# Splitting the P·V matmuls of a decode attention kernel into four column groups, with a new input load, an earlier w2 load and filler matmuls

## The chip, the cores and the metric

The kernel runs on one core of a Trainium2 chip. The metric is the device time of one execution in microseconds (us). A run gives several executions of the changed kernel and of the kernel before it on the same chip. "Span" is the time from the first to the last instruction in a profile; in the two profiled executions it is about 1.8 us shorter than the device time.

The engines are PE (TensorE, matmuls), PEld (its weight loads), DVE (VectorE), ACT (ScalarE), POOL (GpSimd) and SP (SyncE, which here issues the transfers).

## The reference

One decode step mixes attention over a cached K and V with a small MLP, through a gate. B = 2 batches, H = 32 heads, 4096 cached positions, head size 128, model size 512, all in bf16.

```
g = sigmoid((x * gate_w).sum(-1))                 # x: 2 x 1 x 512
q = x @ wq                                        # 32 heads of 128
p = softmax(q . k_cache * 128**-0.5)              # k_cache: 2 x 32 x 4096 x 128
a = (p . v_cache) @ wo                            # v_cache the same size as k_cache
b = relu(x @ w1) @ w2                             # w1: 512 x 1376, w2: 1376 x 512
out = g * a + (1 - g) * b                         # 2 x 1 x 512
```

K and V are 134 of the 145 MB that must be read, and each element is used once.

## The kernel before

The 64 (batch, head) problems run as 32 pairs. A pair's two heads lie on the two halves of the 128 partitions. For each pair, DVE multiplies the K tile by q, and PE sums the products over the head size: 16 matmuls against the identity accumulate 128 columns into 8, and DVE sums those. ACT takes the exponential and writes it to PT_sb. Then comes P·V.

```python
def mult(s):                                    # DVE, 4.4 us
    prod = prodpool.tile([P, NC, Dh], bf16, name="prod")
    nc.vector.tensor_tensor(out=prod, in0=k_t.pop(s), in1=q, op=ALU.mult)

def red(s):                                     # PE, 16 matmuls of 512 columns
    for j in range(Dh // RW):
        nc.tensor.matmul(ps, lhsT=ident, rhs=prod[:, :, j * RW : (j + 1) * RW], ...)

def pv(s):                                      # PE, 16 matmuls of 512 columns
    o_ps = opool.tile([M, JB * Dh], fp32, name="o_ps")          # M = 8 rows
    for q in range(NQ):                                          # NQ = 16
        nc.tensor.matmul(
            o_ps,
            lhsT=PT_sb[:, s % PT_SLOTS, q * JB : (q + 1) * JB, :].rearrange("p j t -> p (j t)"),
            rhs=vt[:, q * JB : (q + 1) * JB, :],
            start=(q == 0), stop=(q == NQ - 1),
        )
# evac(s): ACT scales o_ps by gate / softmax sum into osb (fp32)
# comb(s): PE adds the rows of osb with a 0/1 matrix, 4 fp32 matmuls
```

The stationary operand of a P·V matmul has only 8 columns (4 chunks of keys, two heads), so one PE pass over 512 columns of V uses 8 of 128 columns of the array.

The order of issue matters at the end of the run, since the work of an engine is queued in this order:

```python
for s in range(NP + 3):                         # NP = 32
    if s < NP: mult(s)
    if 3 <= s < NP + 2: sums(s - 2)
    if s >= 3: evac(s - 3); comb(s - 3); unpack(s - 3)
    if s < NP: red(s)
    if 1 <= s <= NP: scores(s - 1)
    ...
    if 2 <= s < NP + 2: pv(s - 2)
    if s >= 3: wo_mm(s - 3)
    ...
    load_k(s + 3); load_v(s + 1)
    if s + 1 == NP - 1: load_wo(NG - 1); load_w2()
mlp_o()                                         # 11 matmuls with w2
# then two casts (DVE, ACT) and the output DMA
```

So when the last product (pair 31) is ready, PE still has to do reduction 31, P·V of pairs 29, 30 and 31 with an evacuation and a combination after each, 8 matmuls with wo and 11 with w2.

The softmax here doesn't subtract the row's maximum and nothing guards it: scores larger than these inputs give would overflow.

Of the kernel before, what the change touches and what calls it, by code (L numbers as in the profile page):

```python
# [9 lines left out]
ACT = mybir.ActivationFunctionType  # L10
ALU = mybir.AluOpType
# [6 lines left out]
JB = 4  # L18
PT_SLOTS = 4
# [3 lines left out]
def kernel(  # L23
# [13 lines left out]
    nc = tc.nc  # L37
    bf16 = mybir.dt.bfloat16
# [11 lines left out]
    DC = D // P  # L50
    NC = Sk // HP
    NQ = NC // JB
    M = 2 * JB
    NP = B * H // 2
    NG = H // GH
    GP = GH // 2
# [62 lines left out]
    def load_v(s):  # L119
# [7 lines left out]
        v_t[s] = t  # L127

    load_k(0)
    xT = consts.tile([P, B, DC], bf16, name="xT")  # L130
    nc.sync.dma_start(out=xT, in_=A_x[:, 0, :].rearrange("b (p c) -> p b c", c=DC))
    gwT = consts.tile([P, DC], bf16, name="gwT")
    nc.sync.dma_start(out=gwT, in_=gate_w.rearrange("(p c) -> p c", c=DC))  # L133
    load_wq(0)
    load_k(1)
    load_k(2)
# [1 line left out]

    ident = consts.tile([P, P], bf16, name="ident")
    make_identity(nc, ident[:])  # L140
    sel = consts.tile([M, JB, 32], fp32, name="sel")
    nc.gpsimd.memset(sel, 0.0)
    nc.gpsimd.affine_select(
        out=sel,
        in_=sel,
        compare_op=ALU.not_equal,
        fill=1.0,
        base=0,
        pattern=[[-2, JB], [-1, 2], [0, DA]],
        channel_multiplier=1,  # L150
    )
    half = consts.tile([P, M], fp32, name="half")
    nc.vector.memset(half, 0.0)
    nc.vector.memset(half[:HP, 0::2], 1.0)
    nc.vector.memset(half[HP:, 1::2], 1.0)
    PT_sb = consts.tile([P, PT_SLOTS, NC, 2], bf16, name="PT_sb")
    nc.vector.memset(PT_sb, 0.0)
    umask = consts.tile([P, DA], fp32, name="umask")
    nc.vector.reduce_sum(
# [3 lines left out]
    OT_sb = consts.tile([P, NG, DR, B], bf16, name="OT_sb")  # L163
    w1_sb = consts.tile([P, DC, Dff], bf16, name="w1_sb")
    w2_sb = consts.tile([P, FC, D], bf16, name="w2_sb")
    xb = consts.tile([P, B, DC, HP], bf16, name="xb")
    for b in range(B):
        nc.vector.tensor_copy(  # L168
            out=xb[:, b], in_=xT[:, b, :].unsqueeze(2).to_broadcast([P, DC, HP])
        )  # L170
    gwb = consts.tile([P, DC, P], bf16, name="gwb")
    nc.vector.tensor_copy(out=gwb, in_=gwT.unsqueeze(2).to_broadcast([P, DC, P]))
    a_ps = apool.tile([B, D], fp32, name="a_ps")
    g_sb = consts.tile([P, B], fp32, name="g_sb")
    omg = consts.tile([P, B], fp32, name="omg")
# [1 line left out]
    def make_qb(g):  # L177
        wq = wq_t[g // WQG].rearrange("p c (i t d) -> p c t i d", t=2, d=Dh)
        i0 = (g % WQG) * GP
        qb = qbpool.tile([P, B, GP, Dh], bf16, name="qb")  # L180
        for b in range(B):
            ps = mmp.tile([P, GP * Dh], fp32, name="mm")
            for t in range(2):
                for c in range(DC):
                    nc.tensor.matmul(  # L185
                        ps[t * HP : (t + 1) * HP, :],
                        lhsT=xb[:, b, c, :],
                        rhs=wq[:, c, t, i0 : i0 + GP, :],
                        start=(c == 0),
                        stop=(c == DC - 1),  # L190
                    )
            nc.scalar.copy(out=qb[:, b], in_=ps.rearrange("p (i d) -> p i d", d=Dh))  # L192
        qb_t[g] = qb
# [23 lines left out]
    def scores(s):  # L217
        sc = smalls.tile([P, NC], fp32, name="sc")
        nc.vector.reduce_sum(out=sc, in_=red_t.pop(s), axis=AX.X)  # L219
        for t in range(2):  # L220
            r = slice(t * HP, (t + 1) * HP)
            nc.scalar.activation(  # L222
                out=PT_sb[r, s % PT_SLOTS, :, t],
                in_=sc[r],
                func=ACT.Exp,
                scale=inv_sqrt_dh,
                accum_out=partials[r, s : s + 1],
            )

    def sums(s):  # L230
        gs = gsp.tile([M, 1], fp32, name="gs")
        nc.tensor.matmul(gs, lhsT=half, rhs=partials[:, s : s + 1], start=True, stop=True)  # L232
        rsg = smalls.tile([M, 1], fp32, name="rsg")
        nc.vector.reciprocal(out=rsg, in_=gs)  # L234
        b = pair(s)[1]
        nc.vector.tensor_tensor(out=rsg, in0=rsg, in1=g_sb[:M, b : b + 1], op=ALU.mult)  # L236
        rsg_t[s] = rsg

    def pv(s):
        vt = v_t.pop(s)  # L240
        o_ps = opool.tile([M, JB * Dh], fp32, name="o_ps")
        for q in range(NQ):
            nc.tensor.matmul(  # L243
                o_ps,
                lhsT=PT_sb[:, s % PT_SLOTS, q * JB : (q + 1) * JB, :].rearrange(
                    "p j t -> p (j t)"
                ),
                rhs=vt[:, q * JB : (q + 1) * JB, :],
                start=(q == 0),
                stop=(q == NQ - 1),  # L250
            )
        o_t[s] = o_ps

    def evac(s):
        osb = smalls.tile([M, JB, Dh], fp32, name="osb")
        nc.scalar.activation(  # L256
            out=osb,
            in_=o_t.pop(s).rearrange("m (j d) -> m j d", d=Dh),
            func=ACT.Copy,
            scale=rsg_t.pop(s),  # L260
        )
        osb_t[s] = osb
# [42 lines left out]
    def gate():  # L305
        ps = mmp.tile([P, GP * Dh], fp32, name="mm")
        z = ps[:, :B]
        for c in range(DC):
            nc.tensor.matmul(
                z, lhsT=gwb[:, c, :], rhs=xT[:, :, c], start=(c == 0), stop=(c == DC - 1)  # L310
            )
        ge = consts.tile([P, B], fp32, name="ge")
        nc.scalar.activation(out=ge, in_=z, func=ACT.Exp, scale=-1.0)
        nc.vector.tensor_scalar_add(ge, ge, 1.0)
        nc.vector.reciprocal(out=g_sb, in_=ge)
        nc.vector.tensor_scalar(omg, g_sb, -1.0, 1.0, op0=ALU.mult, op1=ALU.add)
# [3 lines left out]
    def mlp_h():  # L320
        ps = mmp.tile([P, GP * Dh], fp32, name="mm")
        h_ps = ps[:, : FC * B].rearrange("p (f b) -> p f b", b=B)
        w1m = w1_sb[:, :, : FF * P].rearrange("p c (q f) -> p c f q", f=FF)
        for fc in range(FC):
            fs = P if fc < FF else FREM
            for c in range(DC):
                nc.tensor.matmul(  # L327
                    h_ps[:fs, fc, :],
                    lhsT=w1m[:, c, fc, :] if fc < FF else w1_sb[:, c, FF * P :],
                    rhs=xT[:, :, c],  # L330
                    start=(c == 0),
                    stop=(c == DC - 1),
                )
        for b in range(B):
            nc.scalar.activation(
                out=hT[:, b, :FF], in_=h_ps[:, :FF, b], func=ACT.Relu, scale=omg[:, b : b + 1]
            )
            if FREM:
                nc.scalar.activation(
                    out=hT[:FREM, b, FF:],  # L340
                    in_=h_ps[:FREM, FF:, b],
                    func=ACT.Relu,
                    scale=omg[:FREM, b : b + 1],
                )

    W2_CUTS = [0, 4, 8, FF]

    def load_w2():
        if FREM:
            nc.sync.dma_start(out=w2_sb[:FREM, FF, :], in_=B_w2[FF * P :, :])  # L350
        view = B_w2[: FF * P].rearrange("(p f) j -> p f j", f=FF)
        for f0, f1 in zip(W2_CUTS, W2_CUTS[1:]):
            nc.sync.dma_start(out=w2_sb[:, f0:f1, :], in_=view[:, f0:f1, :])

    def mlp_o():
        order = ([FF] if FREM else []) + list(range(FF))
        for f in order:
            fs = P if f < FF else FREM
            nc.tensor.matmul(  # L359
                a_ps,  # L360
                lhsT=hT[:fs, :, f],
                rhs=w2_sb[:fs, f, :],
                start=False,
                stop=(f == order[-1]),
            )

    make_qb(0)
    for s in range(NP + 3):
        if s < NP:
            mult(s)  # L370
        if 3 <= s < NP + 2:
            sums(s - 2)
        if s >= 3:
            evac(s - 3)
            comb(s - 3)
            unpack(s - 3)
        if s < NP:
            red(s)
        if 1 <= s <= NP:
            scores(s - 1)  # L380
        if s == 1:
            gate()
        if s == 2:
            sums(0)
        if 2 <= s < NP + 2:
            pv(s - 2)
        if s >= 3:
            wo_mm(s - 3)
        if s == 14:
            mlp_h()  # L390
        if s % PPG == PPG - 2 and (s + 2) // PPG < NG:
            make_qb((s + 2) // PPG)
        if s == 9:
            load_wq(1)
        if s % PPG == 3 and s < NP - PPG:
            load_wo(s // PPG)
        if s == 5:
            nc.sync.dma_start(out=w1_sb, in_=B_w1.rearrange("(p c) f -> p c f", c=DC))
        load_k(s + 3)
        load_v(s + 1)  # L400
        if s + 1 == NP - 1:
            load_wo(NG - 1)
            load_w2()
    mlp_o()

    res = consts.tile([B, D], bf16, name="res")
    nc.vector.tensor_copy(out=res[:, : D // 2], in_=a_ps[:, : D // 2])
# [32 lines left out]
```

## Time and profile before

| | before |
|---|---|
| median time (16 executions) | 362.88 us (361.46 to 364.41) |
| profiled execution | 362.03 us, span 360.2 us |
| mean granted PE clock | 0.948 |
| last K tile in use by DVE | from 326.1 us |
| last w2 piece landed (issue 331.6 plus 15.7 to landing) | about 347.3 us |

The page of the profile, the busy table and the table of 40 slices of the span (9.0 us each; a digit is the busy share in tenths, PEclk the granted clock in tenths):

```profile
PE 299.3 (83%) x1499; PEld 134.4 (37%) x1499; DVE 175.5 (49%) x156; ACT 50.8 (14%) x175; POOL 1.2 (0%) x8
...
PE   0364999998998966979799999999799999999976
...
PEclk9989899998999995998679999999999999999998
DMA  7999999999999999999999999999999999999930
GB/s 283 440 422 428 435 426 419 431 418 435 427 428 424 412 435 428 428 428 428 424 431 428 427 426 428 426 426 428 429 426 426 431 429 422 428 431 423 396 119 0
```

PE is the busiest engine by its share, but the DMA row is full from the second slice to the 38th, at about 427 GB/s. The Trainium skill, "DMA: Bandwidth & Descriptors" (Specifications), gives 435 GB/s as the fabric ceiling; the slices from the second to the 37th read 412 to 440 GB/s, so the trace agrees to about one per cent. Only the last two slices, 18 us, have little or no DMA.

Groups of instructions, same page (line, engine, operation, shapes, count, busy us and mean ns of one, idle time before and what ended it):

```profile
L201 DVE TENSOR_TENSOR prod<-kt,qb 128x8192 bf16<-128x8192 bf16 x32 | 141.3, 4419 | 75.4 <-DMA kt<-in_A_k_cache_dram 68.4
L208 PE MATMUL red<-prod,ident 128*128 128x512 bf16 x512 | 127.7, 408 | 15.4 <-DVE prod L201 15.4
L243 PE MATMUL o_ps<-vt,PT_sb 128*8 128x512 bf16 x512 | 115.7, 379 | 0.0
```

P·V keeps PE as busy as the reduction does. DVE waits 68 us for K tiles, which says again that the transfers set the pace.

The chain of waits in the last 35 us (start, length, what; read downward in time):

```profile
330.73 3.56 PE red L208 x16
334.29 3.55 PE o_ps L243 x16
...
338.67 1.06 PE comb L271 x8
339.72 3.55 PE o_ps L243 x16
...
344.10 1.06 PE comb L271 x8
345.15 3.56 PE o_ps L243 x16
...
348.79 0.69 ACT osb L256
...
349.52 1.07 PE comb L271 x8
...
351.28 3.00 PE a_ps L297 x8
354.28 2.96 PE a_ps L359 x11
```

No DMA stands in it. Three P·V groups (o_ps) of 3.55 us each, one after the other, and then the matmuls with wo and w2 (a_ps), end ten microseconds after the last byte of input has landed. One window of this tail (columns: window, length, busy us and count for PE, PEld, DVE, ACT, POOL, then the granted clock, DMA share and GB/s) shows the wo matmuls at half clock:

```profile
352.00:353.00 1.00, 1.00 (x4) 0.33 (x3) 0.00 (x0) 0.00 (x0) 0.00 (x0) 0.50 0.00 0
```

### The profile page before, as it was taken

The numbers are of one execution on the slowest core, as the hardware profiler recorded it, in microseconds if no ns is written. First come the engines' busy times: TensorE is split into PE (matmuls) and PEld (weight loads), VectorE is DVE, ScalarE is ACT, GpSimd is POOL, SyncE is SP. The second block draws the span as 40 slices with busy tenths as digits, with TensorE's granted clock in tenths as the row PEclk, the third lists the DMA queues.
The fourth block names the chain that finished last, engine by engine and source line by source line (L and its number), as shares of the span: only waits on it lengthen the run. The fifth ranks groups of instructions, "written<-read, shape, count | busy, mean of one in ns | idle before, by whom it ended". The sixth has DMA issues, their size and how long they took to land.

```text
span 360.2 us, 3587 instructions
## 1 busy us (share of the span) xinstructions
PE 299.3 (83%) x1499; PEld 134.4 (37%) x1499; DVE 175.5 (49%) x156; ACT 50.8 (14%) x175; POOL 1.2 (0%) x8
## 2 busy tenths in 40 slices
PE   0364999998998966979799999999799999999976
PEld 0121344433444422435334444444344444444332
DVE  1286565561556514564415565556553555565100
ACT  1001011112111100110301111111211111111110
POOL 1000000000000000000000000000000000000000
PEclk9989899998999995998679999999999999999998
DMA  7999999999999999999999999999999999999930
GB/s 283 440 422 428 435 426 419 431 418 435 427 428 424 412 435 428 428 428 428 424 431 428 427 426 428 426 426 428 429 426 426 431 429 422 428 431 423 396 119 0
DMA packets 12115, 145.65 MB, mean 404 GB/s; under 512 B 1634, under 2 KB 1732, under 8 KB 3140
## 3 DMA queue, kind: packets, MB, share of 16 engines
q1 hardware_dynamic: 12100, 145.43, 95.8%
q8 instruction: 11, 0.18, 0.2%
q14 instruction: 4, 0.03, 0.0%
HBM read 145.43 MB, written 0.00 MB: 404 GB/s over the span
## 4 chain that ended last, share of the span: by engine, by line
PE 60%; DMA 27%; DVE 7%; ACT 5%; issue 1%; SPq 0%; ACTq 0%; DVEq 0%
PE red L208 25%; DMA kt<-in_A_k_cache_dram 23%; PE o_ps L243 23%; PE comb L271 7%; DVE prod L201 6%; ACT osb L256 4%; DMA wq<-in_A_wq_dram 3%; PE mm L185 2%; PE a_ps L297 2%; ACT qb L192 1%; PE a_ps L359 1%; PE mm L327 1%; PE gs L232 0%; DVE sc L219 0%; SPq L133 0%
## 5 line engine op out<-in xcount | busy, mean ns | idle before, releaser
L201 DVE TENSOR_TENSOR prod<-kt,qb 128x8192 bf16<-128x8192 bf16 x32 | 141.3, 4419 | 75.4 <-DMA kt<-in_A_k_cache_dram 68.4
L208 PE MATMUL red<-prod,ident 128*128 128x512 bf16 x512 | 127.7, 408 | 15.4 <-DVE prod L201 15.4
L243 PE MATMUL o_ps<-vt,PT_sb 128*8 128x512 bf16 x512 | 115.7, 379 | 0.0
L208 PEld LDWEIGHTS <-ident 128*128 128x128 bf16 x512 | 50.9, 103 | 83.8 <-issue 37.5
L243 PEld LDWEIGHTS <-PT_sb 128*8 128x8 bf16 x512 | 41.9, 87 | 70.4 <-issue 12.7
L271 PE MATMUL comb<-osb,sel 8*32 8x128 f32 x256 | 34.6, 275 | 24.4 <-ACT osb L256 24.4
L256 ACT ACTIVATE osb<-o_ps,rsg 8x512 f32<-8x512 f32 x32 | 21.7, 678 | 198.3 <-PE gs L232 177.5
L234 DVE RECIPROCAL rsg<-gs 8x1 f32<-8x1 f32 x32 | 4.9, 153 | 74.0 <-PE gs L232 74.0
L271 PEld LDWEIGHTS comb<-osb,sel 8*32 8x32 f32 x256 | 24.8, 106 | 28.7 <-ACT osb L256 26.7
L222 ACT ACTIVATE PT_sb<-sc 64x64 bf16<-64x64 f32 x64 | 17.5, 274 | 55.5 <-DVE sc L219 55.1
L185 PE MATMUL mm<-wq,xb 128*64 128x512 bf16 x64 | 10.5, 455 | 17.4 <-DMA wq<-in_A_wq_dram 13.9
L219 DVE TENSOR_REDUCE sc<-red 128x64 f32<-128x512 f32 x32 | 21.6, 675 | 1.0 <-PE red L208 1.0
L185 PEld LDWEIGHTS <-xb 128*64 128x64 bf16 x64 | 4.8, 125 | 21.7 <-issue 11.5
L222 ACT ACTIVATION_READ_ACCUMULATOR PT_sb<-sc 64x1 f32 x64 | 11.8, 185 | 0.0
L192 ACT CAST qb<-mm 128x512 bf16<-128x512 f32 x8 | 4.7, 586 | 33.1 <-PE mm L185 33.1
L297 PE MATMUL a_ps<-wo,OT_sb 128*2 128x512 bf16 x32 | 8.7, 420 | 0.7 <-DVE OT_sb L289 0.7
L232 PEld LDWEIGHTS gs<-partials,half 128*8 128x8 f32 x64 | 5.4, 90 | 9.2 <-issue 2.1
L285 DVE TENSOR_TENSOR tmp<-comb,umask 128x128 f32<-128x128 f32 x8 | 2.3, 287 | 13.4 <-PE comb L271 13.4
L232 PE MATMUL gs<-partials,half 128*8 128x1 f32 x64 | 6.1, 165 | 0.0
L236 DVE TENSOR_TENSOR rsg<-rsg,g_sb 8x1 f32<-8x1 f32 x32 | 4.7, 147 | 1.1
L297 PEld LDWEIGHTS <-OT_sb 128*2 128x2 bf16 x32 | 2.8, 89 | 5.4 <-issue 1.1
L168 DVE COPY xb<-xT 128x256 bf16<-128x256 bf16 x2 | 0.5, 288 | 6.9 <-DMA xT<-in_A_x_dram 6.9
(30 smaller groups left out, 18.8 us busy)
## 6 DMA issues: line engine op xcount, KB each, us to landing
kt<-in_A_k_cache_dram SPq DMA_DIRECT2D x32, 2048.0 KB, 23.2
vt<-in_A_v_cache_dram SPq DMA_DIRECT2D x31, 2048.0 KB, 19.3
wq<-in_A_wq_dram SPq DMA_DIRECT2D x2, 2048.0 KB, 18.8
wo<-in_A_wo_dram SPq DMA_DIRECT2D x4, 1024.0 KB, 16.5
vt<-in_A_v_cache_dram SPq DMA_DIRECT2D x2, 1024.0 KB, 10.6
w_sb<-in_B_w_dram SPq DMA_DIRECT2D x1, 1376.0 KB, 22.6
w_sb<-in_B_w_dram SPq DMA_DIRECT2D x2, 512.0 KB, 15.1
w_sb<-in_B_w_dram SPq DMA_DIRECT2D x1, 256.0 KB, 15.7
```

What stands on the lines that cost most here:

```text
L185: nc.tensor.matmul(ps[t * HP : (t + 1) * HP, :], lhsT=xb[:, b, c, :], rhs=wq[:, c, t, i0 : i0 + GP, :], start=(c == 0), stop=(c == DC - 1),)
L192: nc.scalar.copy(out=qb[:, b], in_=ps.rearrange("p (i d) -> p i d", d=Dh))
L201: nc.vector.tensor_tensor(out=prod, in0=k_t.pop(s), in1=q, op=ALU.mult)
L208: nc.tensor.matmul(ps, lhsT=ident, rhs=prod[:, :, j * RW : (j + 1) * RW], start=(j == 0), stop=(j == Dh // RW - 1),)
L219: nc.vector.reduce_sum(out=sc, in_=red_t.pop(s), axis=AX.X)
L222: nc.scalar.activation(out=PT_sb[r, s % PT_SLOTS, :, t], in_=sc[r], func=ACT.Exp, scale=inv_sqrt_dh, accum_out=partials[r, s : s + 1],)
L232: nc.tensor.matmul(gs, lhsT=half, rhs=partials[:, s : s + 1], start=True, stop=True)
L234: nc.vector.reciprocal(out=rsg, in_=gs)
L243: nc.tensor.matmul(o_ps, lhsT=PT_sb[:, s % PT_SLOTS, q * JB : (q + 1) * JB, :].rearrange("p j t -> p (j t)"), rhs=vt[:, q * JB : (q + 1) * ...
L256: nc.scalar.activation(out=osb, in_=o_t.pop(s).rearrange("m (j d) -> m j d", d=Dh), func=ACT.Copy, scale=rsg_t.pop(s),)
L271: nc.tensor.matmul(ps[32 * i : 32 * (i + 1), :], lhsT=sel[:, j, :], rhs=osb[:, j, :], start=(j == 0), stop=(j == JB - 1),)
L297: nc.tensor.matmul(a_ps, lhsT=OT_sb[:, g, r, :], rhs=wo[:, r, :], start=(g == 0 and r == 0), stop=False,)
```

## The change

The main intent is to run the P·V matmuls four at a time: matmul q writes rows 32k to 32k+31 of the output, k = q mod 4, which is meant to put four matmuls side by side into four column groups of the array. PT_sb is laid out with 32 columns per chunk (8 used, 24 zero), the evacuation covers 128 partitions, and the combination contracts over all 128 rows.

```diff
-    PT_sb = consts.tile([P, PT_SLOTS, NC, 2], bf16, name="PT_sb")
+    PT_sb = consts.tile([P, PT_SLOTS, NQ, CG], bf16, name="PT_sb")      # CG = 32
@@ pv(s)
-        o_ps = opool.tile([M, JB * Dh], fp32, name="o_ps")
+        o_ps = opool.tile([P, JB * Dh], fp32, name="o_ps")
         for q in range(NQ):
+            k = q % NCG                                                  # NCG = 4
             nc.tensor.matmul(
-                o_ps,
-                lhsT=PT_sb[:, s % PT_SLOTS, q * JB : (q + 1) * JB, :].rearrange(...),
+                o_ps[k * CG : (k + 1) * CG, :],
+                lhsT=PT_sb[:, s % PT_SLOTS, q, :],
                 rhs=vt[:, q * JB : (q + 1) * JB, :],
-                start=(q == 0), stop=(q == NQ - 1),
+                start=(q < NCG), stop=(q >= NQ - NCG),
```

Three smaller parts come with it. The input x and the gate vector are loaded as three long rows on the ACT queue and transposed by PE, in place of 384 packets of eight bytes on the SP queue:

```diff
-    xT = consts.tile([P, B, DC], bf16, name="xT")
-    nc.sync.dma_start(out=xT, in_=A_x[:, 0, :].rearrange("b (p c) -> p b c", c=DC))
-    ... the same for gate_w
+    x_sb = consts.tile([B + 1, D], bf16, name="x_sb")
+    nc.scalar.dma_start(out=x_sb[:B], in_=A_x[:, 0, :])
+    nc.scalar.dma_start(out=x_sb[B : B + 1], in_=gate_w.unsqueeze(0))
+    ... four transposes and a copy to xT
```

The first four w2 pieces are loaded ahead of the last wo and multiplied before the wo matmuls (and the 96-row remainder of w2 becomes an overlapping 128-row piece with zeros in hT). Filler matmuls are placed ahead of the last three reductions, to hold the clock:

```diff
+        if s == NP + 2:
+            mlp_o(0, 4, False)
+        if WARM0 <= s < NP:                       # WARM0 = 29
+            warm(WARM_N)                          # WARM_N = 6
@@
         if s + 1 == NP - 1:
+            load_w2(0, 4)
             load_wo(NG - 1)
-            load_w2()
-    mlp_o()
+            load_w2(4, FC)
+    mlp_o(4, FC, True)
```

The order of the q projection's matmuls (the two column halves now alternate) also changes.

More of the change, by code (lines that the diff above doesn't have):

```diff
@@ L52 @@
     NQ = NC // JB
-    M = 2 * JB
+    CG = 32
+    NCG = P // CG
     NP = B * H // 2
@@ L129 @@
     load_k(0)
-    xT = consts.tile([P, B, DC], bf16, name="xT")
-    nc.sync.dma_start(out=xT, in_=A_x[:, 0, :].rearrange("b (p c) -> p b c", c=DC))
-    gwT = consts.tile([P, DC], bf16, name="gwT")
-    nc.sync.dma_start(out=gwT, in_=gate_w.rearrange("(p c) -> p c", c=DC))
+    x_sb = consts.tile([B + 1, D], bf16, name="x_sb")
+    nc.scalar.dma_start(out=x_sb[:B], in_=A_x[:, 0, :])
+    nc.scalar.dma_start(out=x_sb[B : B + 1], in_=gate_w.unsqueeze(0))
     load_wq(0)
@@ L140 @@
     make_identity(nc, ident[:])
-    sel = consts.tile([M, JB, 32], fp32, name="sel")
+    sel = consts.tile([P, JB, CG], fp32, name="sel")
     nc.gpsimd.memset(sel, 0.0)
-    nc.gpsimd.affine_select(
-        out=sel,
-        in_=sel,
-        compare_op=ALU.not_equal,
-        fill=1.0,
-        base=0,
-        pattern=[[-2, JB], [-1, 2], [0, DA]],
-        channel_multiplier=1,
-    )
-    half = consts.tile([P, M], fp32, name="half")
+    for k in range(NCG):
+        nc.gpsimd.affine_select(
+            out=sel[k * CG : (k + 1) * CG],
+            in_=sel[k * CG : (k + 1) * CG],
+            compare_op=ALU.not_equal,
+            fill=1.0,
+            base=0,
+            pattern=[[-2, JB], [-1, 2], [0, DA]],
+            channel_multiplier=1,
+        )
+    xt_ps = combp.tile([P, DC, 4], bf16, name="comb")
+    for c in range(DC):
+        nc.tensor.transpose(
+            xt_ps[:, c, : B + 1], x_sb[:, c::DC], ident[: B + 1, : B + 1]
+        )
+    xT = consts.tile([P, DC, B + 1], bf16, name="xT")
+    nc.vector.tensor_copy(out=xT, in_=xt_ps[:, :, : B + 1])
+    xb = consts.tile([P, B, DC, HP], bf16, name="xb")
+    for b in range(B):
+        nc.vector.tensor_copy(
+            out=xb[:, b], in_=xT[:, :, b : b + 1].to_broadcast([P, DC, HP])
+        )
+    gwb = consts.tile([P, DC, P], bf16, name="gwb")
+    nc.vector.tensor_copy(out=gwb, in_=xT[:, :, B : B + 1].to_broadcast([P, DC, P]))
+    half = consts.tile([P, P], fp32, name="half")
     nc.vector.memset(half, 0.0)
@@ L165 @@
     w2_sb = consts.tile([P, FC, D], bf16, name="w2_sb")
-    xb = consts.tile([P, B, DC, HP], bf16, name="xb")
-    for b in range(B):
-        nc.vector.tensor_copy(
-            out=xb[:, b], in_=xT[:, b, :].unsqueeze(2).to_broadcast([P, DC, HP])
-        )
-    gwb = consts.tile([P, DC, P], bf16, name="gwb")
-    nc.vector.tensor_copy(out=gwb, in_=gwT.unsqueeze(2).to_broadcast([P, DC, P]))
     a_ps = apool.tile([B, D], fp32, name="a_ps")
@@ L182, in make_qb @@
             ps = mmp.tile([P, GP * Dh], fp32, name="mm")
-            for t in range(2):
-                for c in range(DC):
+            for c in range(DC):
+                for t in range(2):
                     nc.tensor.matmul(
@@ L222, in scores @@
             nc.scalar.activation(
-                out=PT_sb[r, s % PT_SLOTS, :, t],
-                in_=sc[r],
+                out=PT_sb[r, s % PT_SLOTS, :, t : 2 * JB : 2],
+                in_=sc[r].rearrange("p (q j) -> p q j", j=JB),
                 func=ACT.Exp,
@@ L230, in sums @@
     def sums(s):
-        gs = gsp.tile([M, 1], fp32, name="gs")
+        gs = gsp.tile([P, 1], fp32, name="gs")
         nc.tensor.matmul(gs, lhsT=half, rhs=partials[:, s : s + 1], start=True, stop=True)
-        rsg = smalls.tile([M, 1], fp32, name="rsg")
+        rsg = smalls.tile([P, 1], fp32, name="rsg")
         nc.vector.reciprocal(out=rsg, in_=gs)
         b = pair(s)[1]
-        nc.vector.tensor_tensor(out=rsg, in0=rsg, in1=g_sb[:M, b : b + 1], op=ALU.mult)
+        nc.vector.tensor_tensor(out=rsg, in0=rsg, in1=g_sb[:, b : b + 1], op=ALU.mult)
         rsg_t[s] = rsg
@@ L240, in pv @@
         vt = v_t.pop(s)
-        o_ps = opool.tile([M, JB * Dh], fp32, name="o_ps")
+        o_ps = opool.tile([P, JB * Dh], fp32, name="o_ps")
         for q in range(NQ):
+            k = q % NCG
             nc.tensor.matmul(
-                o_ps,
-                lhsT=PT_sb[:, s % PT_SLOTS, q * JB : (q + 1) * JB, :].rearrange(
-                    "p j t -> p (j t)"
-                ),
+                o_ps[k * CG : (k + 1) * CG, :],
+                lhsT=PT_sb[:, s % PT_SLOTS, q, :],
                 rhs=vt[:, q * JB : (q + 1) * JB, :],
-                start=(q == 0),
-                stop=(q == NQ - 1),
+                start=(q < NCG),
+                stop=(q >= NQ - NCG),
             )
@@ L254, in evac @@
     def evac(s):
-        osb = smalls.tile([M, JB, Dh], fp32, name="osb")
+        osb = smalls.tile([P, JB, Dh], fp32, name="osb")
         nc.scalar.activation(
@@ L309, in gate @@
             nc.tensor.matmul(
-                z, lhsT=gwb[:, c, :], rhs=xT[:, :, c], start=(c == 0), stop=(c == DC - 1)
+                z, lhsT=gwb[:, c, :], rhs=xT[:, c, :B], start=(c == 0), stop=(c == DC - 1)
             )
@@ L324, in mlp_h @@
         for fc in range(FC):
-            fs = P if fc < FF else FREM
             for c in range(DC):
                 nc.tensor.matmul(
-                    h_ps[:fs, fc, :],
-                    lhsT=w1m[:, c, fc, :] if fc < FF else w1_sb[:, c, FF * P :],
-                    rhs=xT[:, :, c],
+                    h_ps[:, fc, :],
+                    lhsT=w1m[:, c, fc, :] if fc < FF else w1_sb[:, c, Dff - P :],
+                    rhs=xT[:, c, :B],
                     start=(c == 0),
@@ L335, in mlp_h, with load_w2, mlp_o, warm @@
             nc.scalar.activation(
-                out=hT[:, b, :FF], in_=h_ps[:, :FF, b], func=ACT.Relu, scale=omg[:, b : b + 1]
+                out=hT[:, b, :], in_=h_ps[:, :, b], func=ACT.Relu, scale=omg[:, b : b + 1]
             )
-            if FREM:
-                nc.scalar.activation(
-                    out=hT[:FREM, b, FF:],
-                    in_=h_ps[:FREM, FF:, b],
-                    func=ACT.Relu,
-                    scale=omg[:FREM, b : b + 1],
-                )
-    W2_CUTS = [0, 4, 8, FF]
-    def load_w2():
-        if FREM:
-            nc.sync.dma_start(out=w2_sb[:FREM, FF, :], in_=B_w2[FF * P :, :])
-        view = B_w2[: FF * P].rearrange("(p f) j -> p f j", f=FF)
-        for f0, f1 in zip(W2_CUTS, W2_CUTS[1:]):
-            nc.sync.dma_start(out=w2_sb[:, f0:f1, :], in_=view[:, f0:f1, :])
-    def mlp_o():
-        order = ([FF] if FREM else []) + list(range(FF))
+        if FREM:
+            nc.vector.memset(hT[: P - FREM, :, FF:], 0.0)
+    def load_w2(f0, f1):
+        if f1 == FC and FREM:
+            nc.sync.dma_start(out=w2_sb[:, FF, :], in_=B_w2[Dff - P :, :])
+            f1 = FF
+        view = B_w2[: FF * P].rearrange("(p f) j -> p f j", f=FF)
+        cuts = [f0, f1] if f1 < FF else [f0, FF - 2, FF]
+        for c0, c1 in zip(cuts, cuts[1:]):
+            nc.sync.dma_start(out=w2_sb[:, c0:c1, :], in_=view[:, c0:c1, :])
+    def mlp_o(f0, f1, last):
+        order = list(range(f0, f1))
+        if FREM and f1 == FC:
+            order = [FF] + order[:-1]
         for f in order:
-            fs = P if f < FF else FREM
             nc.tensor.matmul(
                 a_ps,
-                lhsT=hT[:fs, :, f],
-                rhs=w2_sb[:fs, f, :],
+                lhsT=hT[:, :, f],
+                rhs=w2_sb[:, f, :],
                 start=False,
-                stop=(f == order[-1]),
+                stop=(last and f == order[-1]),
+            )
+    WARM0, WARM_N = 29, 6
+    def warm(n):
+        ps = mmp.tile([P, GP * Dh], fp32, name="mm")
+        for k in range(n):
+            nc.tensor.matmul(
+                ps, lhsT=ident, rhs=w1_sb[:, 0, :512], start=(k == 0), stop=(k == n - 1)
             )
@@ L375 @@
             comb(s - 3)
+        if s == NP + 2:
+            mlp_o(0, 4, False)
+        if s >= 3:
             unpack(s - 3)
+        if WARM0 <= s < NP:
+            warm(WARM_N)
         if s < NP:
```

## The prediction

> **What bounds the kernel now.** The table of 40 slices shows the DMA engines full from about 3 us to 344 us, at 425 to 435 GB/s; 145.4 MB at 427 GB/s is 340 us. The Trainium skill, "DMA: Bandwidth & Descriptors" (Specifications), gives 435 GB/s as the fabric ceiling; the trace agrees. So PE's 83% busy share is not the limit in the middle: DVE waits 68 us for K tiles (list of waits). The limit changes only at the end. The last K tile lands at 326.1; the last w2 piece lands at about 347.3 (issue plus time to landing), but the span ends at 360.2. The chain of waits from 289 us on is PE: after the last reduction (ends 334.3) it runs three P·V groups of 3.55 us each, with evacuation (0.69) and combination (1.06) between them, then 8 wo and 11 w2 matmuls in 5.96 us, partly at a granted clock of 0.50 (windows of the tail, 352 to 355 us), then 0.82 us of casts and 2.1 us of output DMA.
>
> **What the change does.**
> 1. P·V goes to four 32-column groups. Evidence that groups overlap: the eight q matmuls on two 64-column halves take 1.06 us at full clock (timeline, 252.7), not 8 x 0.222 = 1.78. Estimate for P·V: 4 x 0.216 + 0.2 = 1.1 us, up to 1.6 if the 16 weight loads (87 ns each) limit, against 3.55. The Trainium skill, "TensorE: Matmul & The Clock Gate" (small-M row of the closing table), gives 2.38x for three tiles. In the middle this buys nothing, since DMA is full: PE idles more, and its clock will fall more often (before, 0.948 mean; idle of 4 us was followed by 0.50).
> 2. The last three P·V groups shorten by some 2.2 us each, so V 31's landing (about 339.5 to 340) becomes what P·V 31 waits for, not PE order: it moves from 345.1 to about 340, and combination 31 ends near 343 instead of 350.6.
> 3. The first four w2 pieces are loaded before wo and multiplied early; they hide in the wait. 7 w2 matmuls stay after wo.
> 4. Evacuation over 128 partitions, combination over K=128: free size unchanged, so 0.69 and 1.06 us unchanged.
> 5. Head: 384 eight-byte packets go (285 GB/s at 7 to 8 us), wq is issued 0.96 us earlier. Worth 0.5 to 1 us of the full DMA stream.
> 6. Warm matmuls (18) run in waits. Overlapping 128-row w2 remainder: 32 KB more, 0.1 us.
>
> **Sum.** DMA end: 347.3 - 0.7 = about 346.6. wo lands near 343.5; from there 15 matmuls, half of them cold (3.4 us) and the rest warm, end at 347.3 (warm) to 349 (cold); I take 348.3. Plus 2.96 us of casts and output: span 351.3, down 8.9 us. Time: about 353.3 us, range 350.5 to 356.8. Faster by over 2%: 0.80; within 2%: 0.18; slower: 0.02.
>
> **What would show each step.** P·V busy time per group near 1.1 to 1.6 us; PE share far down (near 60%) with DMA slices unchanged at 425 to 430 GB/s; mean granted clock below 0.948; idle of PE before P·V 31 released by the V DMA; end of DMA within 1 us of 346.6; the chain of waits in its last 20 us naming DMA (V, wo or w2) instead of P·V; wq landing about 0.5 to 1 us earlier.
>
> **What would make it wrong.** Column groups that do not overlap (then under 1%); a cold PE in the middle that lets DMA run dry through late buffer release; w2 or wo landing later than assumed, since the tail pieces flow at only 350 GB/s and one slow DMA queue drags; wo and w2 matmuls all cold (+2 us); or a head gain larger than 1 us.

## The result, and the profile after

| | before | after |
|---|---|---|
| median time | 362.88 us (16 executions, 361.46 to 364.41) | 352.82 us (11 executions, 352.64 to 353.13) |
| profiled execution | 362.03 us, span 360.2 | 353.21 us, span 351.4 |
| mean granted PE clock | 0.948 | 0.874 |
| last K product starts | 326.1 us | 326.1 us |
| last w2 piece landed | about 347.3 us | about 346.9 us |

The ratio is 0.9722 (95% interval 0.9706 to 0.9739). A ratio here is always the mean time of one kernel's fast runs over that of the other's of the same rounds, so it is not quite the ratio of the medians.

The page after, the same lines:

```profile
PE 250.8 (71%) x1521; PEld 116.2 (33%) x1521; DVE 176.1 (50%) x158; ACT 51.0 (15%) x173; POOL 2.2 (1%) x11
...
PE   0364889498485962857799696785884887787685
...
PEclk9989889979789896896789789886998798899899
DMA  7999999999999999999999999999999999999992
GB/s 291 435 431 425 431 423 429 423 427 431 426 425 432 412 428 427 428 428 423 433 425 427 428 429 425 419 439 423 425 433 425 429 429 423 431 429 420 426 411 80
```

The DMA row is as full as before, now to the 39th of 40 slices: the empty stretch at the end is nearly gone. PE and its clock both fell in the middle.

```profile
L209 DVE TENSOR_TENSOR prod<-kt,qb 128x8192 bf16<-128x8192 bf16 x32 | 141.5, 4424 | 134.7 <-DMA kt<-in_A_k_cache_dram 120.3
L216 PE MATMUL red<-prod,ident 128*128 128x512 bf16 x512 | 149.0, 457 | 63.6 <-DVE prod L209 63.6
L252 PE MATMUL o_ps<-vt,PT_sb 128*32 128x512 bf16 x512 | 34.3, 382 | 0.0
```

P·V fell from 115.7 to 34.3 us of busy time, 3.4 times less, though one matmul takes as long as ever (382 ns): four of them overlap. The reduction, untouched by the change, rose from 127.7 to 149.0 us: PE idled more and was granted less clock (0.874 instead of 0.948). An experiment below that keeps PE 39 us busier in the same kernel raises the clock to 0.971 and brings the reduction to 123.2 us.

The chain of waits at the end:

```profile
326.12 4.44 DVE prod L209
...
330.60 5.30 PE red L216 x16
335.90 1.01 PE o_ps L252 x16
...
337.73 0.73 PE comb L278 x5
338.46 1.22 PE o_ps L252 x13
...
340.51 0.73 PE comb L278 x5
341.24 1.21 PE o_ps L252 x12
...
343.27 0.73 PE comb L278 x5
...
345.04 1.89 PE a_ps L304 x8
346.92 1.52 PE a_ps L361 x7
...
348.47 0.42 DVE res L424
```

From the last K product on (326.1 in both) one can subtract step by step. The reduction takes 5.30 instead of 3.56 us (+1.7). P·V takes 1.01 + 1.22 + 1.21 instead of 3.55 + 3.55 + 3.56 (−7.2). The combinations overlap the next group's start (−0.7). The wo matmuls take 1.89 instead of 3.00, since the clock is full there now (−1.1). The w2 matmuls after them take 1.52 instead of 2.96, for four of the eleven moved ahead, and the others run at full clock (−1.4). The sum is −8.7 us, and the spans differ by 8.8. In these two executions everything won is won after the last K tile.

The reduction began at full clock and fell to half of it after about a microsecond. These windows of the profile after show it; the column before the last two is the clock, which stayed at 0.50 to 0.53 until 335:

```profile
330.00:331.00 1.00, 0.40 (x2) 0.19 (x2) 0.97 (x4) 0.00 (x0) 0.00 (x0) 1.00 1.04 442
331.00:332.00 1.00, 1.00 (x5) 0.44 (x4) 0.42 (x1) 0.53 (x4) 0.00 (x0) 0.77 1.06 451
332.00:333.00 1.00, 1.00 (x4) 0.30 (x2) 0.00 (x0) 0.16 (x2) 0.00 (x0) 0.50 0.85 360
```

The medians differ by 10.1 us, 1.2 more than the profiled executions. The profiled execution of the kernel before was one of its quicker ones; that of the kernel after was the slowest of its twelve (353.21; the table leaves it out of the eleven). So the slow reduction above need not be typical of the kernel after: in other runs below with the same tail it ran at full clock. The times before spread over 3 us, those after over 0.5. In the runs of before beside the first experiments, the spans are 358.7 and 359.0 us where the mean clock was 0.961 and 0.962, and 362.0 to 362.5 us where it was 0.943 or 0.944. That fits a last chain made almost only of PE work, which a lost clock lengthens; the link is read from the lists of runs and was not tested by itself.

### The profile page after: what moved, and what is told of

Same layout as the page of the kernel before. It is cut to its first block, busy times and chain, and to the rows that moved or that the text cites. A ratio compares the mean times of both kernels' runs of the same rounds, so it can differ in the third digit from the quotient of the medians.

```text
span 351.4 us, 3637 instructions
## 1 busy us (share of the span) xinstructions
PE 250.8 (71%) x1521; PEld 116.2 (33%) x1521; DVE 176.1 (50%) x158; ACT 51.0 (15%) x173; POOL 2.2 (1%) x11
## 4 chain that ended last, share of the span: by engine, by line
DMA 64%; PE 18%; DVE 14%; ACT 2%; issue 0%; SPq 0%; ACTq 0%; DVEq 0%
DMA kt<-in_A_k_cache_dram 61%; DVE prod L209 14%; PE red L216 11%; DMA wq<-in_A_wq_dram 4%; PE o_ps L252 2%; PE comb L278 2%; PE mm L193 1%; ACT osb L263 1%; PE mm L333 1%; PE a_ps L304 1%; ACT qb L200 1%; PE a_ps L361 0%; PE gs L240 0%; DVE rsg L242 0%; ACT hT L341 0%
## 5 line engine op out<-in xcount | busy, mean ns | idle before, releaser
L216 PE MATMUL red<-prod,ident 128*128 128x512 bf16 x512 | 149.0, 457 | 63.6 <-DVE prod L209 63.6
L216 PEld LDWEIGHTS <-ident 128*128 128x128 bf16 x512 | 57.2, 113 | 149.0 <-issue 114.7
L278 PE MATMUL comb<-osb,sel 128*32 128x128 f32 x256 | 34.8, 280 | 17.1 <-ACT osb L263 17.1
L263 ACT ACTIVATE osb<-o_ps,rsg 128x512 f32<-128x512 f32 x32 | 22.0, 687 | 121.6 <-PE o_ps L252 121.6
L252 PE MATMUL o_ps<-vt,PT_sb 128*32 128x512 bf16 x512 | 34.3, 382 | 0.0
L278 PEld LDWEIGHTS comb<-osb,sel 128*32 128x32 f32 x256 | 25.8, 111 | 20.3 <-ACT osb L263 19.4
L252 PEld LDWEIGHTS <-PT_sb 128*32 128x32 bf16 x512 | 11.7, 95 | 19.1 <-issue 12.3
L240 PEld LDWEIGHTS gs<-partials,half 128*128 128x128 f32 x64 | 9.8, 192 | 13.7 <-issue 13.1
L242 DVE RECIPROCAL rsg<-gs 128x1 f32<-128x1 f32 x32 | 5.2, 163 | 17.3 <-PE gs L240 17.3
L240 PE MATMUL gs<-partials,half 128*128 128x1 f32 x64 | 12.3, 262 | 0.0
```

What stands on the lines that cost most here:

```text
L240: nc.tensor.matmul(gs, lhsT=half, rhs=partials[:, s : s + 1], start=True, stop=True)
L242: nc.vector.reciprocal(out=rsg, in_=gs)
L252: nc.tensor.matmul(o_ps[k * CG : (k + 1) * CG, :], lhsT=PT_sb[:, s % PT_SLOTS, q, :], rhs=vt[:, q * JB : (q + 1) * JB, :], start=(q < NCG) ...
L263: nc.scalar.activation(out=osb, in_=o_t.pop(s).rearrange("m (j d) -> m j d", d=Dh), func=ACT.Copy, scale=rsg_t.pop(s),)
L278: nc.tensor.matmul(ps[32 * i : 32 * (i + 1), :], lhsT=sel[:, j, :], rhs=osb[:, j, :], start=(j == 0), stop=(j == JB - 1),)
```

## The experiments

The theory after the result: the transfers pace everything up to the last K tile, and the gain is the shorter PE chain behind it, nearly all from P·V. The rivals: the head (fewer small packets), the w2 order, the filler matmuls, or a lighter PE load along the whole run.

### Column groups alone

The kernel before, with the layout, P·V, sums, evacuation and combination of the change; head, w2 order and end as before; no filler.

```diff
 # before.py +
+        o_ps = opool.tile([P, JB * Dh], fp32, name="o_ps")
+            k = q % NCG
+                o_ps[k * CG : (k + 1) * CG, :],
+                lhsT=PT_sb[:, s % PT_SLOTS, q, :],
```

> The kernel before with the four column groups for P·V alone (old head, old w2 order, no warm matmuls). Theory (the gain is the shorter compute tail after the last K product, nearly all of it from P·V): the last three P·V groups shrink from 10.7 to about 3.4 us, the last reduction runs partly cold (+1.7 us, no warm matmuls to prevent it), wo and w2 matmuls cost 4.3 to 6 us; time 354 to 357 us, ratio to before 0.976 to 0.983, and the last K tile lands at 326 as in both kernels. Rival (the head with its 384 fewer packets, or the earlier w2 load and the warm matmuls, bring most of it): ratio above 0.99.

Measured: 353.67 us median (353.11 to 354.30, 6 executions), ratio 0.9742 (0.9707 to 0.9778). The last K product started at 326.3. In the chain of waits of its profiled (slowest) execution:

```profile
330.78 5.29 PE red L210 x16
336.07 1.01 PE o_ps L246 x16
...
347.09 2.39 PE a_ps L360 x11
```

So the column groups alone give 9.5 us (363.20 − 353.67, the medians of these rounds) of the 10.1 us of the whole change, a little more than expected. The median is still 0.85 us above that of the changed kernel; what that is made of is taken up under "No filler matmuls".

### All but the column groups

```diff
 # after.py, pv(s)
-            k = q % NCG
+            k = 0
-                start=(q < NCG), stop=(q >= NQ - NCG),
+                start=(q == 0), stop=(q == NQ - 1),
 # and evac, comb over 32 rows
```

> The changed kernel with P·V back in one column group, all else of the change kept. Theory: P·V groups take 3.55 us again and the tail is bound by PE order; only the four early w2 matmuls (0.9 to 1.7 us) are won: time 360 to 362 us, ratio to before 0.992 to 0.998. Rival (head, w2 order or warm matmuls are the cause): about 353 to 356 us, ratio under 0.982.

Measured: 363.17 us median (361.55 to 365.60), ratio 1.0016 (0.9969 to 1.0062): nothing is left, not even the little the theory gave to the w2 order. The chain of waits has its P·V groups back:

```profile
337.38 3.57 PE o_ps L252 x16
...
342.83 3.57 PE o_ps L252 x16
```

The filler matmuls do harm here, since PE was not idle: each batch of six takes 1.4 us of the chain, and the last reduction begins at 333.9 instead of 330.7. From the end of that reduction to the end of the last w2 matmul this run takes 20.5 us, the kernel before 23.0 (there wo and part of w2 ran at half clock). So two effects of 2.4 and 3.2 us nearly cancel, and the run shows that the rest of the change as it stands gains nothing without the groups, not that each part of it is worth nothing. A run without groups and without filler was not made.

### The old head

The loads of x and gate_w of the kernel before, in the changed kernel.

```diff
 # after.py
-    nc.scalar.dma_start(out=x_sb[:B], in_=A_x[:, 0, :])
-    ... transposes
+    nc.sync.dma_start(out=xT, in_=A_x[:, 0, :].rearrange("b (p c) -> p b c", c=DC))
```

> The changed kernel with the old loads of x and the gate vector (384 packets of eight bytes on the SP queue, no PE transposes). Theory: the DMA stream is full either way and the last K tile landed at 326.1 in both kernels, so the head buys nothing that lasts: within 0.4 us of the changed kernel (352.6 to 353.3 us). Rival (the prediction's step 5, 0.5 to 1 us of the DMA stream): 353.4 to 354 us with the last K tile 0.5 to 1 us later.

Measured: 352.86 us (352.67 to 353.11), ratio 0.9720, the same as with the new head (352.82). The last K product started at 326.2. The new head is worth nothing that lasts.

This run's profile shows more. Its last reduction ran at full clock (3.61 us), and then PE waited twice for transfers, in the middle of P·V 31 and before the matmuls with wo (timeline, cut off at 346; in brackets the idle time before and what ended it):

```profile
341.00 0.61 PE L246 MATMUL o_ps<-vt,PT_sb 128*32 128x512 bf16 x8 [0.56 <-DMA vt<-in_A_v_cache_dram]
344.73 1.46 PE L298 MATMUL a_ps<-wo,OT_sb 128*2 128x512 bf16 x6 [0.79 <-DMA wo<-in_A_wo_dram]
```

### w2 loaded and multiplied late

```diff
 # after.py
-            load_w2(0, 4)
             load_wo(NG - 1)
-            load_w2(4, FC)
+            load_w2(0, FC)                        # pieces 0-4, 4-8, 8-10
-        if s == NP + 2:
-            mlp_o(0, 4, False)
-    mlp_o(4, FC, True)
+    mlp_o(0, FC, True)
```

> The changed kernel with all w2 pieces loaded after wo and all eleven w2 matmuls at the end, as before. Theory: 4 matmuls move from a wait into the final chain: +0.9 us if warm, +1.7 us if cold: 353.7 to 354.6 us. Rival (the final chain is bound by the landing of the last w2 piece, not by PE): no change, under 353.2 us.

Measured: 352.96 us median; five executions lie from 352.77 to 353.07 and the profiled one is at 353.84. The theory expected 353.7 or more, and only the profiled execution shows that. In it the reduction took 5.30 us and PE bounded the tail, so the four extra matmuls counted in full (2.39 us for w2 instead of 1.52). The quicker ones were not profiled. By its number the rival was met (under 353.2); whether also by its reason, the landing of the last w2 piece, no profile shows. In the profile wo, no longer behind 512 KB of w2, landed at 343.2 us (issue 325.9 plus 17.3), while in three runs with the early w2 it landed at 344.4 to 344.7 and was what PE waited for (the old head above, two runs below). What the early w2 saves in matmuls it seems to give back in a later wo.

### Two column groups instead of four

```diff
 # after.py, pv(s)
-            k = q % NCG
+            k = q % 2
 # start, stop, evac and comb for 64 rows
```

> The changed kernel with P·V in two column groups instead of four. Theory (the saved time is three P·V groups on the tail): a group takes 8 x 0.216 + 0.2 = 1.9 us instead of 1.05, so the tail is up to 2.6 us longer, less what it now waits for wo (up to 1 us): 354 to 356 us, P·V busy near 62 us in all. Rival (two groups are enough since then the landing of wo and w2 binds): 352.6 to 353.5 us.

Measured: 354.25 us (353.96 to 354.40), ratio 0.9737. The chain of waits:

```profile
330.61 3.61 PE red L216 x16
334.22 1.85 PE o_ps L252 x16
```

A group takes 1.85 us. Here the reduction ran at full clock: the heavier P·V costs 2.1 us more over three groups, and the clock gave 1.7 us of it back. Another 0.7 us goes because the combinations no longer overlap the next group (1.06 us each in the chain, as before); with it 1.1 of the 1.2 us between the two profiled executions are accounted for. Two groups bring 87% of the gain of four, by the medians (363.89 − 354.25 = 9.6 of the 11.1 us to the median of the run without filler below, which shared the chip and the executions of the kernel before).

### No filler matmuls

```diff
 # after.py
-        if WARM0 <= s < NP:
-            warm(WARM_N)
```

> The changed kernel without its 18 warm matmuls. Theory: they end more than 2 us before the last product is ready, so they hold the clock only in some executions; without them the last reduction runs cold in all or most (5.3 us instead of 3.6): 353.0 to 354 us, no more than 1.2 us slower. Rival A (they do nothing): equal within 0.2 us. Rival B (they are what makes the tail fast): over 354.5 us.

Measured: 352.82 us (352.44 to 353.33), ratio 0.9699. Not slower than the expected range, but below it: as fast as with them. The reduction of its profiled execution was still cold (5.05 us). Taken out alone, the filler does nothing that can be measured (rival A).

That is not the same as being worth nothing. Taking out the early w2 alone (352.96), the filler alone (352.82) or the new head alone (352.86) costs at most 0.14 us, but the run with column groups alone, which lacks all three (and the new order of the q projection), is 0.85 us slower (353.67). Its profiled execution has both the slow reduction (5.29 us) and all eleven w2 matmuls at the end (2.39 us). That the early w2 and the filler stand in for one another is likely from this; a run without just these two was not made.

### More filler

```diff
-    WARM0, WARM_N = 29, 6
+    WARM0, WARM_N = 29, 15
```

> The changed kernel with 15 warm matmuls instead of 6 before each of the last three reductions, so that PE works until the last product is ready. Theory: the last reduction takes 3.6 us at full clock in every execution, the chain then waits for wo (landing near 344.5) and ends near 348.1 instead of 348.45: 352.4 to 352.9 us, 0 to 0.4 us faster than the changed kernel and with less spread. Rival (the tail is PE work alone): the full 1.7 us are won, 351.1 to 351.6 us.

Measured: 353.09 us median in two clumps: 352.57, 352.69 and 352.80, and 353.39, 353.94 and 353.98. The profiled execution is of the second clump, and its chain of waits says why the expectation failed:

```profile
329.35 3.35 PE mm L374 x15
332.69 3.45 PE red L216 x16
```

The reduction ran at full clock (3.45 us), but behind its filler: three batches in a row made each pair late, and it began at 332.7 though the product was ready at 330.2. Filler on the engine that is about to be needed is a cost like any other work.

### One batch of filler, where it fits

```diff
-    WARM0, WARM_N = 29, 6
+    WARM0, WARM_N = 31, 15
```

> The changed kernel with one batch of 15 warm matmuls before the last reduction alone (none before the two ahead of it). In the run of three batches of 15 the reduction was at full clock but started 2.1 us late, behind them. Theory: now the batch ends at about 330.3, the reduction takes 3.6 us from 330.6, and the chain meets the landing of wo near 344.5: 352.4 to 352.8 us. Rival (PE alone bounds the tail): 351.2 to 351.6 us.

Measured: 352.69 us median (352.58 to 352.75, with one execution at 353.78), ratio 0.9721. The reduction took 3.6 us at full clock, from 331.5 (still a microsecond behind its filler). Now the chain of waits ends in a transfer:

```profile
327.74 16.62 DMA wo<-in_A_wo_dram
...
344.39 1.89 PE a_ps L304 x8
```

PE was ready and waited 0.45 us for wo. Of the 1.7 us saved in the reduction, 0.9 went into its later start (331.5 instead of 330.6), and wo set the rest: its matmuls began 0.65 us earlier than in the profile of the changed kernel. The median is the theory's number, against the rival's 351.2 to 351.6.

### A PE chain as short as it could be made

The last K product in two halves, so that the reduction starts on the first; six filler matmuls ahead of it only; wo ahead of all of w2.

```diff
 # after.py with "w2 late", WARM0, WARM_N = 31, 6, and in mult(s):
+        cuts = [0, Dh] if s < NP - 1 else [0, Dh // 2, Dh]
+        for d0, d1 in zip(cuts, cuts[1:]):
+            nc.vector.tensor_tensor(out=prod[:, :, d0:d1], in0=kt[:, :, d0:d1], in1=q[:, :, d0:d1], ...)
```

> The changed kernel with everything done to shorten its PE chain: the last K product in two halves so that the last reduction starts 2.2 us earlier, one batch of 6 warm matmuls before it, wo ahead of all w2 pieces, all w2 matmuls at the end. The PE chain alone would end 3 us earlier. Theory (the landing of the last w2 piece, 346.8 to 347.3, is the next limit): 352.2 to 352.7 us. Rival (still PE): 350 to 351.5 us.

Measured: 353.12 us (352.97 to 353.27), ratio 0.9725. This is a miss for both. The reduction ended at 333.6 instead of 335.9, but the chain of waits now holds the V tile of pair 31:

```profile
327.30 13.67 DMA vt<-in_A_v_cache_dram
...
341.01 0.64 PE o_ps L257 x8
```

Its second half landed at 341.0, and from there evacuation, combination, wo and all eleven w2 matmuls follow without a wait for w2. So it was not the last w2 piece that bound, as the theory had it, but V 31. The old head above already had this wait, until 341.0, and the fp32 run below has it until 340.8. Three limits lie within a microsecond of each other: V 31 and what hangs on it, the landing of wo, and the PE chain of the changed kernel. Shortening one hands over to the next.

### More PE work in the middle, three times

First P·V of pairs 0 to 23 three times over:

```diff
-        for q in range(NQ):
+        for r, q in [(r, q) for r in range(3 if s < 24 else 1) for q in range(NQ)]:
```

> The changed kernel with P·V of the first 24 pairs done three times over (the last time counts; result unchanged), so that PE has about its old load in the middle. Theory (DMA is the limit there): within 0.5 us of the changed kernel (352.4 to 353.4 us) though PE is busy some 45 us longer, and the last K tile lands at 326 as ever; the mean clock rises toward 0.95. Rival (part of the gain comes from lighter PE work along the whole run): 355 us or more.

Measured: 354.24 us (353.90 to 354.45), ratio 0.9736: 1.4 us slower than the changed kernel, between theory and rival. The last K product started at 327.7 instead of 326.1. PE was busy 24.7 us longer rather than 45, since the reduction ran less cold. The page showed one more difference: six more packets on the queue that carries instructions (18 instead of 12). The next two runs part the load on PE from the number of its instructions. One adds PE work with few instructions, three fp32 matmuls a pair:

```diff
+    def load_pe(osb):
+        for k in range(3):
+            nc.tensor.matmul(ps, lhsT=half, rhs=osb, start=(k == 0), stop=(k == 2))
```

> The changed kernel with three extra float32 matmuls of 512 columns in each of pairs 0 to 23 (results unused): more PE time in the middle than the tripled P·V added, but only some 6 extra instructions a pair instead of 64. Theory (PE load in the middle costs nothing; the 1.4 us of the tripled run came with its 1,536 extra instructions, whose fetches share the DMA engines): 352.4 to 353.2 us, last K product at 326. Rival (PE load in the middle does cost): 354 us or more, last K product at 327.5 or later.

Measured: 352.72 us (352.65 to 352.81), ratio 0.9714, the last K product at 326.0. The busy table of its page:

```profile
PE 289.6 (83%) x1665; PEld 136.5 (39%) x1665; DVE 176.8 (50%) x158; ACT 51.0 (15%) x173; POOL 2.2 (1%) x11
```

PE is busy 39 us more than in the changed kernel, with a mean clock of 0.971, and the time is the same. PE load in the middle costs nothing here. The other adds instructions with little work, 32 matmuls of two columns a pair:

```diff
+    def many(n):                                  # n = 32
+        for k in range(n):
+            nc.tensor.matmul(ps[:, :2], lhsT=ident, rhs=ident[:, :2], ...)
```

> The changed kernel with 32 tiny matmuls (two columns each, results unused) in each of pairs 0 to 23: as many extra PE instructions (1,536) as the tripled P·V had, with no V reads behind them. Theory (the 1.4 us of the tripled run came with its instructions, fetched over the same DMA engines: that run moved 0.09 MB more): 353.8 to 354.6 us, last K product near 327.5, about 145.79 MB in all. Rival (it came from the work of the tripled P·V): 352.5 to 353.2 us, last K product at 326.

Measured: 354.07 us (353.72 to 354.34), ratio 0.9742, the last K product at 327.4. The table of DMA queues (packets, MB, share of 16 engines) of the changed kernel, then of this one:

```profile
q8 instruction: 12, 0.20, 0.2%
```

```profile
q8 instruction: 18, 0.29, 0.3%
```

The Trainium skill, "Runtime: NRT & Kernel Launch" (Instruction fetch mechanics), says that instructions are refilled in blocks of 16 KiB, 256 instructions each, at a cost that is mostly hidden. 1,536 more instructions (768 matmuls and as many weight loads) are six such blocks, and the trace has six more packets. Both runs with these instructions are slower, by 1.3 and 1.4 us, and the run with more PE work but few more instructions is not: the time goes with the number of instructions, not with the work. That their packets delay K is not shown, and the traces speak against a plain sum. The six packets had all passed by 280 us, and in this run the product of pair 30 still started at 316.3, only 0.3 us later than in the changed kernel. The other 1.0 us came with the last K tile alone (issued at 301.2, in use at 327.4; in the changed kernel 300.9 and 326.1), while no extra packet passed. How the instructions cost this microsecond stays open.

## Why the prediction was right

The forecast was 353.3 us, from 350.5 to 356.8, faster by over 2%; 352.82 was measured. Point by point:

- *What bounds the kernel.* Right. The middle is paced by transfers: 39 us of extra PE work there change nothing, and the last K product starts at 326.1 before and after. The tail was PE work: it is where all of the gain of the profiled pair lies.
- *Step 1, P·V at 1.1 to 1.6 us.* Right, at its low end: 1.05 us for a group in the timeline, 1.01 to 1.22 us in the chain. The overlap read from the q projection's two halves (1.06 us for eight matmuls) carried over to four groups. The Trainium skill, "TensorE: Matmul & The Clock Gate" (small-M row of the closing table), has 2.38 times for three tiles; here four give 3.4 times in busy time, and two give 1.9 times (3.55 to 1.85).
- *Step 2, V 31 becomes what P·V 31 waits for.* Wrong in the profiled run, by the reduction. The prediction had it at 3.6 us and warned of a cold PE only in the middle and in the wo and w2 matmuls; it took 5.30 us, most of it at half clock. So P·V 31 started at 341.2, not 340, and combination 31 ended at 344.3, not 343, both in PE's own order. Where the reduction ran at full clock, the step came true: P·V 31 waited for the second half of V 31 until 341.0 (old head), 340.8 (fp32 matmuls) and 341.0 (short chain), about a microsecond later than forecast, and combination 31 ended at 343.5 and 343.3 in the first two. How many executions of the changed kernel are of this kind is not known, since only its slowest was profiled.
- *Step 3, early w2 hides in the wait.* The matmuls did leave the last chain, but with the filler in place the time gained is 0.1 us at the median, less than the spread, and wo then lands 1.2 to 1.5 us later.
- *Step 4, evacuation and combination unchanged.* Right: 0.69 us; a combination still takes 1.06 us, though 0.33 of it now overlaps the next matmuls.
- *Step 5, 0.5 to 1 us from the head.* Wrong. wq was ready 0.2 us earlier, the last K product not at all, and putting the old head back changes nothing (352.86).
- *Step 6, filler.* Its effect was left open in the sum; taken out alone, it is nil.
- *The sum.* wo at 343.5 plus 4.8 us of matmuls gave 348.3; the profile has 345.0 plus 3.4, ending at 348.45. Start and length were off by 1.5 us each, in opposite directions: the start for the cold reduction or, where that was warm, for wo landing at 344.4 to 344.7 (seen in three runs); the length because PE was at full clock at the very place where half of it had been feared cold. The agreement to half a microsecond is partly luck; the range was the honest part.
- *Signs named.* P·V time, the lower clock (0.874), the unchanged DMA rate and the end of DMA (346.9, forecast 346.6) came as said. PE's share fell to 71%, not near 60%; the colder reduction (21 us, 6% of the span) is the larger part of that. The chain of waits of the profiled execution names PE, not a DMA; with a reduction at full clock it names wo in four runs (old head, fp32 matmuls, many small matmuls, one batch of filler) and V 31 in the short chain.

No version tried is faster than the changed kernel by more than 0.13 us (352.69 with one batch of filler, within its spread), so it was left as it is. Its last input lands near 346.9, and at least the last matmuls with w2, 0.8 us of casts and 2.1 us of output follow.

## What to carry to other kernels

In a kernel whose transfers are full, look for PE time not in its busy share but behind the last large tile: in this kernel each microsecond of the serial chain counted there, until the next transfer bound, and 39 us in the middle did not count at all. A matmul with a narrow stationary operand is the first candidate there, since writing it to separate 32-row groups of the output cost only layout here (evacuation and combination stayed at 0.69 and 1.06 us). When one chain is shortened, expect the neighbours (the clock, the next landing) to take part of it back, and read them off before spending work on filler or reordering. A part that costs nothing when taken out alone may still stand in for another: take them out together too.

## What the Trainium skill lacked or had wrong

- "Runtime: NRT & Kernel Launch" (Instruction fetch mechanics) calls the cost of crossing a 16 KiB block mostly hidden. Where transfers are the limit, six more blocks (1,536 small PE instructions) went with 1.3 us: 354.07 against 352.82 us, with the last K product 1.3 us later. That fetching them is the cause is not shown, so this does not refute the page.
- "TensorE: Matmul & The Clock Gate" (Part 3 and the closing table) has 2.38 times for three column tiles and no measured figure for two or four at 128 rows of contraction, nor has any other page. Here 16 matmuls of 512 columns took 3.55 us in one group, 1.85 in two and 1.05 in four.
- The same page (closing table) advises no PE-idle gaps over some 3 us. The length of one gap did not decide: after a gap of 2.2 us the reduction of the changed kernel began at full clock and fell to 0.50 a microsecond later (5.30 us), and after a gap of 3.2 us that of the run with many small matmuls stayed at full clock (3.61 us). Its Part 1, which has a free-running window, would fit this better; no run here tests the window.
- The same page tells of clock lost to waiting, but not what that means for a change that takes work from PE: the matmuls that are left can get slower. The mean time of a reduction matmul rose from 408 to 457 ns when P·V became shorter, and 1.7 us of the gain were lost that way in the profiled execution.
